# Local attention with a mixture-of-experts step: how many transfers of SyncE's queue are under way at once

## The chip, the cores and the metric

The kernel runs on one core of one Trainium2 chip. A core has TensorE (PE), VectorE (DVE), ScalarE (ACT), GpSimd (POOL) and SyncE (SP), each with its own stream of instructions, and 16 DMA engines that move data between memory (HBM) and the core's SBUF. The metric is device time in microseconds (us) of one execution; less is better.

## The reference

Eight batches of eight heads, 576 positions, head size 64. Attention looks back over 63 positions and the own one. Its output, seen as 576 rows of 512 per batch, is the input of the second part: a gate score per row, the 128 rows of the highest score in each batch go through two dense layers, and the result is added to these rows.

```python
scores = scale * np.matmul(q, k.transpose(0, 1, 3, 2))
mask = (rel >= 0) & (rel < 64)          # rel = query position - key position
attn = softmax(np.where(mask, scores, -1e9))
x = np.matmul(attn, v)                  # then (B, S, H * D): 8, 576, 512
scores = np.einsum('bsd,d->bs', x, w_gate)
for b in range(B):
    top_idx = np.argpartition(-scores[b], 128)[:128]
    xe = x[b, top_idx]
    ye = np.maximum(xe @ w1, 0.0) @ w2  # 512 -> 1024 -> 512
    g = 1.0 / (1.0 + np.exp(-scores[b, top_idx]))
    out[b, top_idx] = x[b, top_idx] + g[:, None] * ye
```

## The kernel before

**Attention.** The 8 x 576 positions are cut into windows of 64, and two windows make one block: 36 blocks of 128 positions with all heads. Block m needs one load of q, one of k and one of v (256 KB each; a k that straddles two batches is two loads of 128 KB). `attend(m)` makes of it: 32 PE instructions of scores (tile s), on DVE the mask and the row maximum (p, nm), on ACT the exponential (p), on PE 8 transposes (t), on ACT the copies to SBUF (pt), on PE the product with v (av, some 60 instructions), on ACT and DVE the division (z, x), on DVE the gate's scalar product, and one store of the 128 rows (x to out_dram, 256 KB; two of 128 KB where a block straddles two batches).

**Mixture of experts.** When the last block of a batch is done, `choose(b)` ranks its 576 scores: PE transposes the scores (r), DVE compares them all with each other, PE sums (lo) and makes the row indices (ix), and POOL gathers the 128 chosen rows from out_dram (xe, an indirect DMA). `moe(gi)` runs the two layers for one or two batches: transposes of the gathered rows (xt), the first layer (hp), transposes of its result (ht), the second layer (yp), the gated sum, and a scatter by POOL. Its weights are split into a high and a low part: `weight(step)` loads one of 16 pieces (st, 256 KB) that POOL splits in two.

**What sets the order.** Nothing in the program is scheduled by the chip's availability at run time: `Order.run` lays all operations out beforehand, engine by engine, by a small model of durations and due times, and emits them in that order; on the chip each engine works its stream off strictly in order, waiting on semaphores. In the model a transfer of SP occupies one common wire (`wire`, `RATE` bytes per us) and lands 1.75 us after its bytes; a transfer isn't issued while the wire is booked more than `BACKLOG` = 3 us ahead:

```python
if op.size and e == "SP":
    t = max(t, wire - BACKLOG)
```

All loads and stores except the first k go through SP's queue, 168 in all. On the chip nothing of this model holds them back: SP issues a transfer as soon as its buffer is free (a q buffer when the scores of an earlier block are done, a store when its x is done) and when its semaphore is free. There are eight semaphores for these transfers, taken in turn (DMAHW0 to DMAHW7; the first k, on ACT's queue, has DMAHW0), so that each transfer waits until the one eight ahead has landed. The loads are written in `load(m)` (`go_q`, `go_k`, `go_k2`, `go_v`), `lwg`, `go_load` and the stores in `go_st`, each as `nc.sync.dma_start`.

Of the kernel before, what the change touches and what calls it, by code (L numbers as in the profile page):

```python
# [12 lines left out]
F32 = _mybir.dt.float32  # L13
# [8 lines left out]
P = 128  # L22
W = 64
# [7 lines left out]
LINK = {"PE": 0.25}  # L31
TURN = 0.15
RATE = 375e3
BACKLOG = 3.0
KEEP = {0: 2, 1: 2, 2: 1}
WARM = 8
DIRECT = (0,)
# [18 lines left out]
class Order:  # L56
# [15 lines left out]
    def add(self, *a, **kw):  # L72
        op = Op(*a, **kw)
        self.ops.append(op)
        return op
# [15 lines left out]
    def run(self, engines, free):  # L91
        for op in self.ops:
            op.left = len(op.after)
            for a, _ in op.after:
                a.then.append(op)
        avail = {e: [] for e in engines}
        for op in self.ops:
            if not op.left:
                avail[op.eng].append(op)
        mode = None  # L100
        wire = 2.0
        done = 0
        self.log = []
        while done < len(self.ops):
            best = None
            for e in engines:
                cand = []
                for op in avail[e]:
                    t, picks = self.ready(op)
                    if t == float("inf"):  # L110
                        continue
                    t = max(t, free[e])
                    if op.size and e == "SP":
                        t = max(t, wire - BACKLOG)
                    cand.append((t, op.due, op, picks))
                if not cand:
                    continue
                t0 = min(c[0] for c in cand)
                same = e == "PE" and mode == 64
                c = min((c for c in cand if c[0] <= t0 + SLACK.get(e, 0.0)  # L120
                         or same and c[2].mode == mode and c[0] <= t0 + STAY),
                        key=lambda c: (same and c[2].mode != mode, c[1]))
                if best is None or c[0] < best[0]:
                    best = c
            assert best is not None, [(e, [o.due for o in avail[e]]) for e in engines]
            t, _, op, picks = best
            if op.mode and mode and op.mode != mode:
                t = max(t, free["PE"] + TURN)
            for (key, kind), n in zip([k for k in op.take if k[0] not in self.where], picks):
                self.where[key] = n  # L130
                self.room[n] = float("inf")
            op.start = t
            if op.mode:
                mode = op.mode
            free[op.eng] = t + op.pitch
            if op.size:
                begin = max(wire, t + op.pitch + 0.25)
                wire = begin + op.size / RATE
                op.end = max(wire, begin + 0.2) + 1.75
            else:  # L140
                op.end = t + op.dur
            for key in op.give:
                self.room[self.where[key]] = op.end + 0.1
            avail[op.eng].remove(op)
            for o in op.then:
                o.left -= 1
                if not o.left:
                    avail[o.eng].append(o)
            self.log.append((t, op))
            op.go()  # L150
            done += 1
# [7 lines left out]
def tile_attention_moe(ctx: ExitStack, tc, q, k, v, wg, w1, w2, outs, B, H, S, D, C):  # L159
    nc = tc.nc  # L160
    E = H * D
    F = w1.shape[1]
    NP = H // 2
# [5 lines left out]
    D1 = D + 1  # L169
    SCALE = 1.0 / np.sqrt(D).item()  # L170
    order = Order()
    add = order.add
# [28 lines left out]
    order.rooms("sel", ["sel0"])  # L201

    serial = [0]

    def make(key, shape, dtype, space="sb", sub=""):
        tag = order.where[key] + sub
        serial[0] += 1
        t = (p_ps if space == "ps" else p_sb).tile(
            shape, dtype, tag=tag, name=f"{key[0]}{sub}{'_'.join(map(str, key[1:]))}")
        order.tiles[key, sub] = t  # L210
        return t

    def get(key, sub=""):
        return order.tiles[key, sub]
# [19 lines left out]
    for opened in (None, 0, 1):  # L234
        m = const.tile([P, 2, W], F32, name=f"mask{len(maskc)}")
        nc.gpsimd.memset(m, 0.0)
        for c in range(2):
            r = slice(c * W, (c + 1) * W)
            nc.gpsimd.affine_select(
                out=m[r, 1, :], in_=m[r, 1, :], pattern=[[-1, W]],  # L240
# [3 lines left out]
            else:  # L244
                nc.gpsimd.affine_select(
                    out=m[r, 0, :], in_=m[r, 0, :], pattern=[[1, W]],
# [57 lines left out]
    wgb = const.tile([P, E], F32, name="wgb")  # L304
# [5 lines left out]
    def at(n, off=0.0):  # L310
        return BEGIN + STEP * n + off
# [9 lines left out]
    def load(m):  # L321
        b, i = divmod(2 * m, NW)
        both = i + 1 == NW
        due = at(m, -9.0)

        def go_q():
            nc.sync.dma_start(make(("q", m), [P, NP, 2, W], F32), q[m])

        def ktile(c):
            if ("k", c) not in order.where or (("k", c), "") not in order.tiles:  # L330
                make(("k", c), [P, NW, NP, W], F32)
            return get(("k", c))

        def go_k():
            eng = nc.scalar if m == 0 else nc.sync
            if not both:
                eng.dma_start(ktile(b)[:, i:i + 2], k[m])
            else:
                eng.dma_start(ktile(b)[:, i], k[m, :, 0])

        def go_k2():
            nc.sync.dma_start(ktile(b + 1)[:, 0], k[m, :, 1])

        def go_v():
            nc.sync.dma_start(make(("v", m), [P, 2, NP, D1], F32), v[m])

        LQ[m] = add("SP", go_q, 0.44, due, take=[(("q", m), "q")], size=P * NP * 2 * W * 4)
        kk = [add("SP", go_k, 0.44, due + 0.01, take=[(("k", b), "k")],
                  size=P * (1 if both else 2) * NP * W * 4)]
        if both:  # L350
            kk.append(add("SP", go_k2, 0.44, due + 0.02, take=[(("k", b + 1), "k")],
                          size=P * NP * W * 4))
        LK[m] = kk
        LV[m] = add("SP", go_v, 0.44, due + (0.03 if m > 1 else 0.6),
                    take=[(("v", m), "vv")], size=P * 2 * NP * D1 * 4)

    for m in range(NM):
        load(m)
    lwg = add("SP", lambda: nc.sync.dma_start(wgb, wg), 0.44, at(1, -7.9), size=P * E * 4)

    w1v = w1.rearrange("(c p) f -> p c f", p=P)
    w2v = w2.rearrange("(c p) e -> p c e", p=P)
    CH = 512
# [3 lines left out]
    def piece(step, t):  # L367
        if step < KC1 * n1:
            j, c = divmod(step, KC1)
            return t[0][:, c, j * CH:(j + 1) * CH]  # L370
        c = (step - KC1 * n1) * n2
        return t[1][:, c:c + n2].rearrange("p a e -> p (a e)")
# [2 lines left out]

    def weight(step):
        def go_load():
            nc.sync.dma_start(make(("st", step), [P, CH], F32), piece(step, (w1v, w2v)))

        def go_hi():  # L380
            nc.gpsimd.tensor_scalar(out=piece(step, (w1h, w2h)), in0=get(("st", step)),
                                    scalar1=1.0, scalar2=1.0, op0=ALU.mult, op1=ALU.mult)

        def go_lo():
            nc.gpsimd.tensor_tensor(
                out=piece(step, (w1l, w2l)), in0=get(("st", step)),
                in1=piece(step, (w1h, w2h)).bitcast(F32), op=ALU.subtract)

        l = add("SP", go_load, 0.44, 12 + 2.2 * step, take=[(("st", step), "h")],
                size=P * CH * 4)  # L390
        WHI[step] = add("POOL", go_hi, 0.62, 16 + 2.2 * step, [l])
        WLO[step] = add("POOL", go_lo, 1.26, 16.1 + 2.2 * step, [WHI[step]],
                        give=[("st", step)])
# [26 lines left out]
    def attend(m):  # L420
# [123 lines left out]
        def xf():  # L544
            return get(("x", m)).rearrange("p j r d -> p (j r d)")
# [10 lines left out]
        b, i = divmod(2 * m, NW)  # L556
# [4 lines left out]

        def go_st(bb, rows, parts):
            def go():
                nc.sync.dma_start(outs[bb][rows, :], xf()[parts])
            return go

        ST[m] = []
# [482 lines left out]
```

## Time and profile before

| | us |
|---|---|
| three runs, median (lowest to highest) | 259.08 (256.22 to 260.87) |
| the profiled execution | 256.81 |
| its span, first to last instruction | 255.1 |
| PE busy in the span | 233.7 |
| DVE busy | 175.4 |
| ACT busy | 157.1 |
| POOL busy | 76.8 |

Busy times are sums over the span; a line number (L512) is that of the kernel before, and a name such as av<-v,pt says what is written from what. The chain that ended last is followed back from the last instruction: at each step to what released it. "issue" in it is time in which an engine waited for nothing that the profile shows. The DMA row has 40 slices of 6.4 us each. A transfer's landing is counted from the start of its issue. A window's row gives, for each engine, busy us and the number of instructions in it.

### The profile page before, as it was taken

Reading aid. Unit: us, or ns where it says so; the run is one execution under the profiler, and the core shown is the slowest. Engines: PE = TensorE matmul, PEld = TensorE weight load, DVE = VectorE, ACT = ScalarE, POOL = GpSimd, SP = SyncE. Lnnn points to the kernel's source line nnn. Section 1 sums busy time; section 2 is a strip of 40 time slices with the busy share of each in tenths; the row PEclk is TensorE's granted clock in tenths of the full one; section 3 lists DMA queues with packets and bytes.
Section 4 is the critical chain, followed back from the end, with each engine's and each line's share of the span. In section 5 each row is a group of like instructions: output and inputs, shape, how many; then the busy total and the mean of one; then the engine's idle time right before and its main releaser. Section 6 shows DMA issues by size and latency. Waiting matters only on the chain.

```text
span 255.1 us, 10922 instructions
## 1 busy us (share of the span) xinstructions
PE 233.7 (92%) x4406; PEld 200.8 (79%) x4406; DVE 175.4 (69%) x911; ACT 157.1 (62%) x451; POOL 76.8 (30%) x117
## 2 busy tenths in 40 slices
PE   8887777987998998999999999999999999999992
PEld 7676756866887887888787878888878899889891
DVE  0588795995797889777997779899765852512210
ACT  2978883974788949777895888799675212101100
POOL 7589967900010025125002500700250030020021
PEclk9999995997999999999999999999999999999998
DMA  7999999984177839943895597363213010011011
GB/s 231 391 387 383 342 319 362 358 309 164 51 237 278 223 117 273 328 127 127 242 344 190 167 326 232 93 183 101 78 66 117 9 58 28 0 44 41 0 44 41
DMA packets 25170, 47.26 MB, mean 185 GB/s; under 512 B 2976, under 2 KB 4000, under 8 KB 25120
## 3 DMA queue, kind: packets, MB, share of 16 engines
q1 hardware_dynamic: 23680, 42.10, 49.4%
q0 software_dynamic: 1296, 4.20, 4.7%
q8 instruction: 35, 0.57, 0.9%
q10 hardware_dynamic: 144, 0.26, 0.3%
q14 instruction: 15, 0.12, 0.1%
HBM read 35.01 MB, written 11.53 MB: 182 GB/s over the span
## 4 chain that ended last, share of the span: by engine, by line
PE 79%; DVE 7%; ACT 5%; issue 4%; DMA 3%; POOLq 0%; ACTq 0%; DVEq 0%
PE yp L965 16%; PE s L430 13%; PE av L512 12%; PE t L468 12%; PE hp L918 9%; PE hp L853 8%; ACT p L460 3%; PE r L615 2%; DMA xe<-out_dram,idx 2%; DVE p L451 2%; PE xt L785 2%; PE wp L221 1%; ACT pt L476 1%; PE ht L882 1%; DMA out_dram<-xe,idxh 1%
## 5 line engine op out<-in xcount | busy, mean ns | idle before, releaser
L460 ACT ACTIVATE p<-p,nm 128x128 f32<-128x128 f32 x288 | 96.3, 398 | 27.1 <-DVE nm L451 27.0
L451 DVE CUSTOM_DVE_ANT_0 p<-s,mask 128x128 f32<-128x128 f32 x288 | 66.1, 282 | 21.4 <-PE s L430 21.1
L512 PE MATMUL av<-v,pt 64*64 64x65 f32 x2176 | 45.0, 225 | 8.8 <-issue 7.1
L512 PEld LDWEIGHTS av<-v,pt 64*64 64x64 f32 x2176 | 41.1, 137 | 12.6 <-issue 9.7
L468 PE MATMUL t<-ident,p 128*128 128x128 f32 x288 | 44.8, 281 | 2.5 <-ACT p L460 1.5
L430 PE MATMUL s<-k,q 64*64 64x128 f32 x1152 | 42.6, 280 | 1.5 <-DVE nm L451 1.1
L430 PEld LDWEIGHTS s<-k,q 64*64 64x64 f32 x1152 | 32.8, 135 | 10.8 <-issue 7.3
L476 ACT COPY pt<-t 128x512 f32<-128x512 f32 x72 | 39.2, 585 | 2.0 <-PE t L468 1.2
L468 PEld LDWEIGHTS t<-ident,p 128*128 128x128 f32 x288 | 32.9, 142 | 7.7 <-ACT p L460 2.5
L997 POOL DMA_INDIRECT out_dram<-xe,idx x7 | 7.9, 1126 | 95.5 <-DVE xe L988 59.5
L414 DVE CUSTOM_DVE_ANT_0 jk<-x,wgb 128x512 bf16<-128x512 f32 x36 | 27.2, 755 | 1.0
L965 PE MATMUL yp<-w2l,hh 128*128 128x512 f32 (+1 forms) x72 | 27.6, 384 | 0.0
L965 PE MATMUL yp<-w2h,hh 128*128 128x512 f32 (+1 forms) x72 | 27.5, 382 | 0.0
L965 PE MATMUL yp<-w2h,hl 128*128 128x512 f32 (+1 forms) x72 | 27.1, 377 | 0.0
L540 DVE TENSOR_TENSOR x<-av,z 128x512 f32<-128x512 f32 x36 | 24.8, 690 | 1.4
L451 DVE DVE_READ_ACCUMULATOR2_ANT nm<- 128x1 f32 x288 | 23.6, 82 | 0.0
L942 ACT ACTIVATE hh<-hp 128x512 fp32r<-128x512 f32 x8 | 4.8, 598 | 28.9 <-PE hp L918 28.9
L760 POOL DMA_INDIRECT xe<-out_dram,idx x8 | 8.8, 1103 | 40.7 <-DVE nm L451 32.3
L532 ACT ACTIVATE z<-av,eps 128x8 f32<-128x8 f32 x36 | 9.4, 260 | 15.0 <-PE av L512 12.3
L918 PE MATMUL hp<-xgh,w1h 128*128 128x256 f32 x64 | 18.2, 284 | 0.0
L918 PE MATMUL hp<-xgh,w1l 128*128 128x256 f32 x64 | 18.2, 284 | 0.0
L918 PE MATMUL hp<-xgl,w1h 128*128 128x256 f32 x64 | 17.9, 280 | 0.0
(97 smaller groups left out, 352.1 us busy)
## 6 DMA issues: line engine op xcount, KB each, us to landing
v<-in_v SPq DMA_DIRECT2D x36, 260.0 KB, 4.0
q<-in_q SPq DMA_DIRECT2D x36, 256.0 KB, 4.3
out_dram<-x SPq DMA_DIRECT2D x32, 256.0 KB, 4.5
k<-in_k SPq DMA_DIRECT2D x31, 256.0 KB, 6.0
st<-in_w SPq DMA_DIRECT2D x16, 256.0 KB, 5.7
k<-in_k SPq DMA_DIRECT2D x8, 128.0 KB, 4.8
out_dram<-x SPq DMA_DIRECT2D x8, 128.0 KB, 4.4
k<-in_k ACTq DMA_DIRECT2D x1, 256.0 KB
```

What stands on the lines that cost most here:

```text
L414: nc.vector.tensor_tensor_reduce(out=junk()[:n, :E], in0=xf[:n], in1=wgb[:n], op0=ALU.mult, op1=ALU.add, scale=1.0, scalar=0.0, accum_out=acc)
L430: nc.tensor.matmul(s[r][c * W:(c + 1) * W, j], get(("q", m))[rs, j, c], keys(m, c, j, rs), start=True, stop=True)
L451: nc.vector.tensor_tensor_reduce(out=get(("p", m))[:, j, :, r], in0=st_s[m][r][:, j], in1=mk, op0=ALU.add, op1=ALU.min, scale=-SCALE, scal ...
L460: nc.scalar.activation(pe[:, j, :, r], pe[:, j, :, r], AF.Exp, bias=st_nm[m][:, r, j:j + 1], scale=-1.0)
L468: nc.tensor.transpose(get(("t", m, a))[:, j, :], get(("p", m))[:, j, a].rearrange("p r w -> p (r w)"), ident)
L476: nc.scalar.copy(pt, get(("t", m, a)))
L512: nc.tensor.matmul(av[cs, r, j * D1:(j + 1) * D1], pt[a][rs, j, cs], get(("v", g // 2))[rs, g % 2, j], start=a == 0 or o == c, stop=a == 1)
L532: nc.scalar.activation(z[:, 0], avv()[:, :, :, D], AF.Identity, bias=eps)
L540: nc.vector.tensor_tensor(out=x.rearrange("p j r d -> p r j d"), in0=avv()[:, :, :, :D], in1=st_z[m][:, 1].unsqueeze(3).to_broadcast([P, 2 ...
L853: nc.tensor.matmul(get(hk)[:C], get(xk, a)[:, c, 0], w[:, c, nb * 512:(nb + 1) * 512], start=(n == 0), stop=(n == 3 * KC1 - 1))
L918: nc.tensor.matmul(get(hk)[:, j], w[:, c, js], get(xk, a)[:, c].rearrange("p u c -> p (u c)"), start=(n == 0), stop=(n == 3 * KC1 - 1))
L965: nc.tensor.matmul(get(yk)[:C, :e1 - e0], get((a, gi, c // per))[:, c % per, u * C:(u + 1) * C], w[:, c, e0:e1], start=(n == 0), stop=(n = ...
```

## The change

From its eleventh transfer on, SP waits before each of its loads and stores until the fourth one ahead on the same queue has landed, so that at most four are under way. The wait is added by hand (`move`), and the planner's model gets the same rule in place of `BACKLOG`. All transfers of SP's queue now go through `move`.

```diff
-BACKLOG = 3.0
+FLIGHT = 4
+FIRST = 10
...
         wire = 2.0
+        flight = []
...
-                    if op.size and e == "SP":
-                        t = max(t, wire - BACKLOG)
+                    if op.size and e == "SP" and len(flight) >= FIRST:
+                        t = max(t, flight[-FLIGHT] + 0.1)
...
                 op.end = max(wire, begin + 0.2) + 1.75
+                if op.eng == "SP":
+                    flight.append(op.end)
...
+    flight = []
+
+    def move(out, in_, eng=None):
+        i = (eng or nc.sync).dma_start(out, in_)
+        if eng is None:
+            if len(flight) >= FIRST:
+                tc.add_manual_dep(
+                    i.ins, flight[-FLIGHT].name,
+                    _mybir.DependencyInfo(_mybir.DependencyClass.Sync,
+                                          _mybir.DependencyReason.DATA),
+                    reason="transfers under way")
+            flight.append(i.ins)
...
-            nc.sync.dma_start(make(("q", m), [P, NP, 2, W], F32), q[m])
+            move(make(("q", m), [P, NP, 2, W], F32), q[m])
```

The other loads and the store are changed like the last two lines.

SP's queue, its tenth to twentieth transfer before the change (q, k, v of a block, st a piece of weights; a number behind a name tells buffers apart), with what each waits for:

```order
L327 DMA q_198<-in_q 128x512 [waits DMAHW2_49]
L337 DMA k_160<-in_k 128x512 [waits DMAHW3_49]
L345 DMA v_215<-in_v 128x520 [waits DMAHW4_49]
L378 DMA st_240<-in_w 128x512 [waits DMAHW5_49]
L378 DMA st_264<-in_w 128x512 [waits DMAHW6_49]
L327 DMA q_278<-in_q 128x512 [waits DMAHW7_49]
L339 DMA k_160<-in_k 128x256 [waits DMAHW0_49]
L342 DMA k_316<-in_k 128x256 [waits DMAHW1_49]
L345 DMA v_323<-in_v 128x520 [waits DMAHW2_49]
L378 DMA st_354<-in_w 128x512 [waits DMAHW3_49]
L378 DMA st_363<-in_w 128x512 [waits DMAHW4_49]
```

The same place of SP's queue after it:

```order
L213 DMA q_254<-in_q 128x512 [waits DMAHW2_49]
L213 DMA k_160<-in_k 128x512 [waits DMAHW7_49,DMAHW3_49]
L213 DMA v_285<-in_v 128x520 [waits DMAHW4_49,DMAHW0_49]
L213 DMA st_312<-in_w 128x512 [waits DMAHW5_49,DMAHW1_49]
L213 DMA st_348<-in_w 128x512 [waits DMAHW6_49,DMAHW2_49]
L213 DMA q_360<-in_q 128x512 [waits DMAHW3_49]
L213 DMA k_160<-in_k 128x256 [waits DMAHW4_49]
L213 DMA k_398<-in_k 128x256 [waits DMAHW5_49]
L213 DMA v_442<-in_v 128x520 [waits DMAHW6_49]
L213 DMA out_dram<-x_369 128x512 [waits DMAHW7_49,DVE_49]
L213 DMA st_462<-in_w 128x512 [waits DMAHW0_49]
```

The tenth transfer waits as before. The eleventh to fourteenth wait for two semaphores, their own (eight ahead) and that of the fourth ahead; from the fifteenth on the fourth ahead is left, since the one eight ahead has been waited for by then. The first store has moved from the 24th to the 19th place. The load of the eighth q (block 7, counted from 0) goes from the 33rd place to the 34th, the last piece of weights from the 59th to the 61st.

PE's stream between the index matmuls (ix) of the second batch and the transposes (xt) of the rows gathered by these indices, its first rows before the change:

```order
L736 MATMUL ix_1609<-posb_137,sel_4_1600 128x2
L468 MATMUL t_0_1619<-ident,p_1488 128x128 [waits PE_49,Activation_49]
L468 MATMUL t_0_1619<-ident,p_1488 128x128 [waits Activation_49] x3
L853 MATMUL hp_1_1399<-w1l,xgh_1114 128x512 [waits Pool_49]
L853 MATMUL hp_1_1399<-w1h,xgl_1115 128x512
L468 MATMUL t_1_1643<-ident,p_1488 128x128 [waits DVE_49]
L468 MATMUL t_1_1643<-ident,p_1488 128x128 x3
L965 MATMUL yp_0_1653<-w2h,hh_0_1432 128x512 [waits Pool_49]
```

and after it:

```order
L754 MATMUL ix_1434<-posb_137,sel_4_1425 128x2
L871 MATMUL hp_1_1376<-w1h,xgh_1088 128x512
L871 MATMUL hp_1_1376<-w1l,xgh_1088 128x512 [waits Pool_49]
L871 MATMUL hp_1_1376<-w1h,xgl_1089 128x512
L983 MATMUL yp_0_1450<-w2h,hh_0_1419 128x512 [waits Activation_49,Pool_49]
L983 MATMUL yp_0_1450<-w2l,hh_0_1419 128x512 [waits Pool_49]
L983 MATMUL yp_0_1450<-w2h,hl_0_1432 128x512 [waits DVE_49]
L983 MATMUL yp_0_1450<-w2h,hh_0_1419 128x512
```

Up to xt there follow, before the change, eight more rows of yp, four transposes ht, the scores of one block and the V product of another. After it, one more of yp, the four of ht, two transposes t, the scores of one block, the V product of another and one transpose t. The rows behind the scores of the last block are the same in both.

## Rows read from the trace of the kernel before

**Rows 1.** The page, busy us of each engine, share of the span, instructions.
```profile
PE 233.7 (92%) x4406; PEld 200.8 (79%) x4406; DVE 175.4 (69%) x911; ACT 157.1 (62%) x451; POOL 76.8 (30%) x117
```

**Rows 2.** The page, GB/s of the DMA engines in 40 slices of 6.4 us.
```profile
GB/s 231 391 387 383 342 319 362 358 309 164 51 237 278 223 117 273 328 127 127 242 344 190 167 326 232 93 183 101 78 66 117 9 58 28 0 44 41 0 44 41
```

**Rows 3.** Chain of work that ended last: start us, us, what.
```profile
15.69 0.99 issue
...
20.38 1.46 issue
...
25.53 1.42 issue
...
56.70 2.38 issue
```

**Rows 4.** Waits of PE, who for whom: us in total, times, longest us.
```profile
PE av L512 <- issue: 7.1, 7, 2.4
...
PE av L512 <- ACT p L460: 1.3, 1, 1.3
...
PE xt L785 <- DMA xe<-out_dram,idx: 1.0, 1, 1.0
```

**Rows 5.** The page, DMA queue 8: packets, MB, share of 16 engines.
```profile
q8 instruction: 35, 0.57, 0.9%
```

**Rows 6.** DMA queue 8 in the windows 24.6 to 24.7, 56.6 to 56.8, 109.8 to 110.0.
```profile
q8 instruction: 1, 0.02, 54.9%
...
q8 instruction: 1, 0.02, 30.1%
...
q8 instruction: 1, 0.02, 31.6%
```

**Rows 7.** Windows: stretch, us, busy us (instructions) per engine, PEclk, DMA share, GB/s.
```profile
20.38:25.53 5.15, 3.69 (x125) 3.28 (x126) 4.42 (x29) 4.01 (x14) 5.15 (x5) 1.00 1.04 381
...
21.84:24.65 2.81, 2.81 (x88) 2.58 (x88) 2.08 (x9) 1.89 (x6) 2.81 (x5) 1.00 1.04 375
59.09:109.90 50.81, 48.55 (x1031) 41.63 (x1031) 41.93 (x221) 39.01 (x113) 7.27 (x8) 0.97 0.63 201
```

**Rows 8.** One q load and one v load on SP: ns of issue, start, landing.
```profile
L327 SPq DMA_DIRECT2D q<-in_q x1: 431/431/431, 21.8 to 21.8; - x1
...
DMA to landing us min/median/max: 5.5/5.5/5.5
...
L345 SPq DMA_DIRECT2D v<-in_v x1: 328/328/328, 170.6 to 170.6; - x1
...
DMA to landing us min/median/max: 2.6/2.6/2.6
```

**Rows 9.** Waits of SP between 5 and 23 us.
```profile
SPq L378 <- DMA v<-in_v: 1.6, 3, 0.7
SPq L345 <- DMA q<-in_q: 0.9, 3, 0.4
```

**Rows 10.** Windows of three attention blocks, and of the stage around 56.7 us.
```profile
14.49:18.79 4.30, 3.31 (x105) 2.93 (x104) 3.75 (x21) 3.52 (x12) 3.80 (x4) 1.00 1.03 389
18.79:23.61 4.82, 3.36 (x106) 2.94 (x105) 4.09 (x21) 3.68 (x12) 4.82 (x6) 1.00 1.06 393
23.61:28.47 4.86, 3.44 (x106) 3.03 (x105) 3.41 (x21) 3.67 (x12) 4.86 (x6) 1.00 1.01 357
55.02:66.58 11.56, 9.18 (x117) 7.90 (x116) 7.08 (x33) 6.93 (x21) 0.00 (x0) 0.85 0.41 140
```

**Rows 11.** Timeline of PE: scores of block 7, start us, us.
```profile
32.04 0.44 PE L430 MATMUL s<-k,q 64*64 64x128 f32 x4
```

**Rows 12.** Chain of work that ended last: a gather, transposes, second-layer matmuls.
```profile
73.27 6.02 DMA xe<-out_dram,idx
...
80.00 0.87 PE t L468 x8
...
88.63 2.09 PE yp L965 x9
```

## What the change does to the time: the prediction

> **What bounds the kernel now.** I read the page first. TensorE (PE) is busy for 92% of the span, VectorE (DVE) 69%, ScalarE (ACT) 62% [rows 1]; matmuls are pipelined, so this alone proves little. The DMA row says that the first 45 us are another stage than the rest: 320 to 390 GB/s once it has begun, later mostly under 300 [rows 2]. Then the chain that ended last. Nearly all of it is PE work, and the few holes in it are the question. The largest are called "issue", time in which PE waited for nothing that the profile shows: 0.99, 1.46 and 1.42 us in the first 27 us and 2.38 us at 56.70, 6.25 us together [rows 3]. In the list of PE's waits they are the first row, 7.1 us before the probability-times-V matmuls; behind it come one wait of 1.3 us put down to ACT and one of 1.0 us for a gather [rows 4]. All other holes have an engine or a gather to name.
>
> What ends the "issue" holes? The loads and stores show a queue of the kind "instruction": 35 packets, 0.57 MB, so 16 KB each [rows 5]. In narrow windows one packet can be placed in time: its share times window times 16 engines is its length. The packet that starts between 24.6 and 24.7 takes 54.9% x 0.1 x 16 = 0.88 us and ends near 25.53, where a hole begins; the one that starts between 56.6 and 56.8 takes 0.96 us and ends near 57.7, inside the hole from 56.70 to 59.09 [rows 3, 6]. In both, PE goes on about 1.4 us after the packet has ended. From the start of one hole to the start of the next, PE did 125 matmuls and 126 weight loads [rows 7], 251 instructions; 16 KB of 64 bytes is 256, and a few semaphore instructions make up the rest. So I read it thus: PE's program arrives in 16 KB blocks, and in the holes PE has run out of instructions.
>
> The Trainium skill (Runtime: NRT & Kernel Launch, section Instruction fetch mechanics) has the same 16 KiB blocks of 256 instructions, and says that crossing to the next one is mostly hidden. The trace agrees on the size, by its 251 instructions, and not on the hiding, by its 6.25 us.
>
> Why are some blocks late? With little else under way the packet came early: one starts between 109.8 and 110.0 us, and by 109.90 PE had done 2062 instructions since the hole that ended at 59.09, which is 8.2 blocks; so the packet started when a fifth of the block in hand was used, and no hole followed. In the crowded stretch, from 21.84 to the packet at 24.65, PE had used 176 of 251, seven tenths [rows 6, 7]. The same request thus waits some microseconds longer when SyncE's (SP's) queue is full. A q load issued at 21.8 took 5.5 us to land; a v load with the queue nearly empty, at 170.6, took 2.6 us [rows 8]. At 391 GB/s one 256 KB transfer takes 0.67 us of the wire [rows 2], and eight of them 5.4 us: the 5.5 us is the queue of eight that the kernel allows itself, since each transfer reuses the semaphore of the one eight ahead (the order's rows on SP). SP waited for such landings all through this stretch [rows 9]. A block that is fetched through an engine with this backlog waits behind it.
>
> **The change, part by part.** (1) *The waits.* From SP's row 11 on, each transfer waits for the one four ahead; most of the old waits, eight ahead, fall away as implied. No instruction is added that computes. Queued behind a waiting transfer are the next loads and stores of SP, nothing else. With four under way the backlog is 4 x 0.67 = 2.7 us, about the lone landing of 2.6 us, so landing falls from 5.5 to between 2.7 and 3.0 us (an estimate: 2.6 us and one issue of SP, 431 ns [rows 8], in front). A block then starts some 2.5 us earlier. The holes of 0.99, 1.46 and 1.42 us need less than that, the 2.38 us just that.
>
> What this is worth is read stage by stage. Three blocks of attention, 14.49 to 28.47, take 13.98 us; PE is busy for only 3.31 to 3.44 us of each, but DVE for 3.75, 4.09 and 3.41 and ACT for 3.52 to 3.68 [rows 10]. Without holes the pace is set by these two, whose work of a block depends on each other; I take 4.0 us a block, 12.0 in all. So 3.87 us of holes give 2.0 us (between 0, if DVE and ACT take it all back, and 2.7, at DVE's mean of 3.75 us a block). In the stage around 56.70 PE has work of its own, 9.18 us in 11.56 us, against 7.08 for DVE [rows 10]: that hole counts nearly whole, 2.2 us (0 to 2.4). The 1.3 us put down to ACT has the same line and comes in the middle of the same matmuls; it could be such a hole or not, so half, 0.6 us (0 to 1.3). The smaller "issue" holes in the row of 7.1 us, 0.9 us beyond the four: 0.2 us (0 to 0.9). Sum 5.0 us (0 to 7.3).
>
> (2) *Does the window starve the transfers?* Four landings in 2.7 to 3.0 us are 0.68 to 0.75 us a transfer instead of 0.67. The tightest use I found is the eighth q load: issued at 21.8, landed 5.5 us later at 27.3, used at 32.04 [rows 8, 11], 4.8 us to spare. It is SP's 34th row after the change, so 23 waits lie before it: 23 x 0.08 = 1.8 us late at the most, inside the 4.8. Cost 0; without that cover, 1.8 us.
>
> (3) *The planner's order.* The planner now believes in later landings, so it moves rows on every engine. The PE work is the same and the rows behind the last attention blocks are the same, so only covers change. The one I can price: between the index matmuls of the second sequence and the transposes of the rows gathered by them, PE had two first-layer and nine second-layer matmuls and eight transposes of probabilities beside one block's scores and one V product; now it has three, five and three (the order's rows on PE show the first of them). A matmul of these is 2.09 / 9 = 0.23 us, a transpose 0.87 / 8 = 0.11 us [rows 12], so 3 x 0.23 + 5 x 0.11 = 1.2 us of cover is gone, in a place where PE waited 1.0 us for a gather of 6.02 us [rows 4, 12]. A shorter backlog should shorten that gather by about as much. I take a loss of 0.4 us (0 to 1.2). Stores move ahead of weight loads on SP, which costs nothing: they go out once their block is done, and weight pieces are first used long after.
>
> Sum: 5.0 - 0.4 = 4.6 us. The profiled execution took 256.81 us (span 255.1), so 252.2 for one like it; the median of the three is 259.08, 2.3 us above, and one like it would come to 254.5. Holes that depend on the phase of a queue may well differ between executions, so I lean to the lower one: **253.0 us**.
>
> **The rivals.** *The holes close but the time is taken back* by DVE and ACT, by new, shorter holes (a block that meets four transfers still waits 2.7 us, and its last 0.9 + 1.4 us come on top), or by the new order: gain 0 to 3 us, 256 to 259 us. For it: DVE and ACT at 3.5 to 4.1 us of each early block. Against it: the stage at 56.70, where PE alone is short.
>
> *The blocks do not wait behind the transfers.* Then nothing changes but the order: 257 to 260 us. For it, the trace has no row that shows when a block is asked for. Against it, a fifth against seven tenths of a block used. The Trainium skill (DMA: Bandwidth & Descriptors, section Queues, rings and completion order) says that an engine goes round its queue rows packet by packet; by that a block would wait for one packet and not for a queue, and the change would give nothing. The late packets in the crowded stretch speak against it here.
>
> *Slower: the window starves the loads.* If landing does not shorten with the depth, four in 4.4 us (towards the middle between 3.0 and 5.5) are 1.1 us a transfer: 23 x (1.1 - 0.67) = 9.9 us late at the eighth block, 4.8 us of it to spare, 5.1 us of waits: 262 us. It decides from 0.67 + 4.8 / 23 = 0.88 us a transfer, 3.5 us for four. Against it: 2.6 us for a lone one.
>
> **How the numbers follow.** The forecast, holes mostly gone and the sum about right: 0.57. Time taken back: 0.25. Blocks not behind the transfers: 0.08. Starved loads: 0.10. A measurement of this kernel can tell about 2% from no change, 5.2 us, so faster means under 253.9. The forecast's own range is 249.5 to 255.5, of which I put 0.9 under 253.9, and a sliver of the second case: faster 0.54. Slower, over 264.3, needs most of the starving or a bad order: 0.07. Same 0.39. The range for 8 in 10 goes from 248.8 (all 7.3 us from the profiled execution, and 0.7) to 259.0.
>
> **What would show it.** Right: no "issue" hole over 0.5 us on PE in the first 60 us; landing of a q load near 22 us about 3 us; a block's packet that starts when less than half of the block in hand is used; the DMA row still near 350 GB/s in the first 40 us; attention blocks of about 4.0 us there. Wrong: holes of the same size with the shorter queue (blocks do not wait behind it); score matmuls that wait for loads, and DMA under 280 GB/s (starved); a gather wait of over 2 us (the order).

## The result: 1.0% slower, with the holes nearly gone

Median 258.75 us over 20 runs (256.49 to 262.70), against 257.62 us over 20 runs of the kernel before (254.06 to 262.86): ratio 1.0104, 95% interval 1.0069 to 1.0139. Executions more than 1.5% above the fastest of the same kernel are left out of the ratios, so a ratio in this text is not the quotient of the medians beside it. The profiled execution has a span of 257.6 us, against 255.1 before.

The page of the kernel after: PE's busy time, the granted clock in 40 slices of 6.4 us in tenths, and the GB/s of the DMA engines (the rows that answer [rows 1, 2]).

```profile
PE 235.6 (91%) x4406; PEld 201.6 (78%) x4406; DVE 175.5 (68%) x911; ACT 157.4 (61%) x451; POOL 76.6 (30%) x117
...
PEclk9999599599999999999999999999999999999999
...
GB/s 237 320 219 253 276 285 245 275 250 281 238 296 270 266 218 189 283 275 198 247 273 224 267 277 285 123 135 121 51 81 84 41 45 41 0 43 41 0 43 41
```

Waits of PE after, who for whom: us in total, times, longest us (these answer [rows 4]).

```profile
PE s L448 <- DMA k<-in_k: 5.5, 3, 3.4
PE t L486 <- ACT p L478: 2.2, 3, 1.0
PE xt L803 <- DMA xe<-out_dram,idx: 1.7, 2, 1.5
...
PE s L448 <- issue: 0.9, 1, 0.9
PE av L530 <- issue: 0.8, 3, 0.3
```

Two things happened at once. The wait for "issue" before the V products fell from 7.1 us [rows 4] to 0.8, none longer than 0.3 us: the holes of [rows 3] are gone. One "issue" wait of 0.9 us is left ahead of score matmuls, at 98.4 us; all rows of "issue" together fell from 7.8 to 1.9 us. And a wait that was not there before stands on top of the list: the score matmuls wait 5.5 us for k loads. The DMA row of the page tells where it comes from: 219 to 285 GB/s from the third to the ninth slice, where it was 309 to 387 [rows 2].

PE's timeline after, between 14 and 27 us: start us, us, what, and in brackets the idle time ahead of it and what ended it.

```profile
14.29 1.10 PE L448 MATMUL s<-k,q 64*64 64x128 f32 x32
...
19.33 0.99 PE L448 MATMUL s<-k,q 64*64 64x128 f32 x27 [1.41 <-DMA k<-in_k]
...
25.75 2.10 PE L448 MATMUL s<-k,q 64*64 64x128 f32 x32 [3.37 <-DMA k<-in_k]
```

Blocks 4 and 5 wait for their k. During the second wait the granted clock falls from 1.00 to a half (1.2 instead of 2.4 GHz), and the same 32 score matmuls take 2.10 us instead of 1.10. (Before, the clock falls once between 10 and 58 us, near 38.6; after, twice, near 24.5 and 45.0.) How the first stage pays for this is one row of each kernel, the window from 10 to 60 us (stretch, us, busy us and instructions of each engine, PEclk, DMA share, GB/s); the kernel before first:

```profile
10.00:60.00 50.00, 40.06 (x1027) 33.75 (x1026) 39.50 (x222) 36.38 (x110) 32.97 (x35) 0.92 0.99 349
```

The same window after:

```profile
10.00:60.00 50.00, 40.17 (x946) 33.92 (x945) 35.47 (x207) 34.63 (x104) 29.60 (x32) 0.86 0.84 259
```

As much busy time, but 946 matmuls instead of 1027, at a clock of 0.86 instead of 0.92, with 259 GB/s instead of 349. Over the whole profiled execution PE's busy time grew by 1.9 us for the same 4406 matmuls, and the sum of the listed waits from 15.8 to 16.3 us; together 2.4 of the 2.5 us by which the spans differ.

By the records of SP's instructions, transfers 11 to 61 are issued between 8.93 and 59.41 us, 50 steps of 1.01 us (before: 11 to 59 between 5.82 and 41.08 us, 48 steps of 0.73 us). How long they took to land stands in the DMA issues of a window (what, count, KB each, median us from issue to landing). The trace has the landing of one transfer in eight only, so each of these medians rests on one or two transfers (from 3.5 to 4.7 us after, from 5.0 to 5.7 before). After, from 10 to 60 us:

```profile
st<-in_w SPq DMA_DIRECT2D x16, 256.0 KB, 4.0
...
k<-in_k SPq DMA_DIRECT2D x7, 256.0 KB, 4.1
out_dram<-x SPq DMA_DIRECT2D x6, 256.0 KB, 3.5
```

and before, from 6 to 41 us:

```profile
st<-in_w SPq DMA_DIRECT2D x15, 256.0 KB, 5.7
...
q<-in_q SPq DMA_DIRECT2D x8, 256.0 KB, 5.2
```

Half as many under way landed in about 0.7 of the time, not in half of it.

### The profile page after: what moved, and what is told of

The parts are those of the page before. It is cut to its first block, busy times and chain, and to the rows that moved or that the text cites. A ratio compares the mean times of both kernels' runs of the same rounds, so it can differ in the third digit from the quotient of the medians.

```text
span 257.6 us, 10912 instructions
## 1 busy us (share of the span) xinstructions
PE 235.6 (91%) x4406; PEld 201.6 (78%) x4406; DVE 175.5 (68%) x911; ACT 157.4 (61%) x451; POOL 76.6 (30%) x117
## 4 chain that ended last, share of the span: by engine, by line
PE 65%; DMA 3%; DVE 2%; issue 2%; ACT 1%; POOLq 0%; ACTq 0%
PE yp L983 16%; PE s L448 10%; PE t L486 9%; PE av L530 9%; PE hp L936 9%; PE hp L871 6%; DMA xe<-out_dram,idx 2%; PE r L633 2%; PE xt L803 1%; DVE p L469 1%; DMA out_dram<-xe,idxh 1%; PE ht L900 1%; PE lo L713 1%; ACT p L478 1%; POOLq L1064 0%
## 5 line engine op out<-in xcount | busy, mean ns | idle before, releaser
L469 DVE CUSTOM_DVE_ANT_0 p<-s,mask 128x128 f32<-128x128 f32 x288 | 66.5, 282 | 31.4 <-PE s L448 31.1
L448 PE MATMUL s<-k,q 64*64 64x128 f32 x1152 | 45.1, 286 | 8.0 <-DMA k<-in_k 5.5
L486 PE MATMUL t<-ident,p 128*128 128x128 f32 x288 | 46.5, 286 | 3.5 <-ACT p L478 2.2
L448 PEld LDWEIGHTS s<-k,q 64*64 64x64 f32 x1152 | 34.6, 139 | 18.3 <-issue 11.1
L530 PE MATMUL av<-v,pt 64*64 64x65 f32 x2176 | 44.4, 226 | 0.9 <-issue 0.8
L530 PEld LDWEIGHTS av<-v,pt 64*64 64x64 f32 x2176 | 41.7, 139 | 3.7 <-issue 2.4
L1015 POOL DMA_INDIRECT out_dram<-xe,idx x7 | 7.3, 1047 | 81.6 <-DVE xe L1006 59.3
L432 DVE CUSTOM_DVE_ANT_0 jk<-x,wgb 128x512 bf16<-128x512 f32 x36 | 26.2, 728 | 1.0
L739 POOL TENSOR_SCALAR sel<-slots,diff 128x128 bf16<-128x128 f32 x20 | 14.6, 735 | 27.6 <-DVE diff L723 26.8
L1006 DVE SCALAR_TENSOR_TENSOR xe<-yp,gs,xe 128x512 f32<-128x512 f32 (+1 forms) x9 | 6.2, 692 | 16.5 <-PE yp L983 16.5
```

Source lines behind the costliest of these rows:

```text
L432: nc.vector.tensor_tensor_reduce(out=junk()[:n, :E], in0=xf[:n], in1=wgb[:n], op0=ALU.mult, op1=ALU.add, scale=1.0, scalar=0.0, accum_out=acc)
L448: nc.tensor.matmul(s[r][c * W:(c + 1) * W, j], get(("q", m))[rs, j, c], keys(m, c, j, rs), start=True, stop=True)
L469: nc.vector.tensor_tensor_reduce(out=get(("p", m))[:, j, :, r], in0=st_s[m][r][:, j], in1=mk, op0=ALU.add, op1=ALU.min, scale=-SCALE, scal ...
L486: nc.tensor.transpose(get(("t", m, a))[:, j, :], get(("p", m))[:, j, a].rearrange("p r w -> p (r w)"), ident)
L530: nc.tensor.matmul(av[cs, r, j * D1:(j + 1) * D1], pt[a][rs, j, cs], get(("v", g // 2))[rs, g % 2, j], start=a == 0 or o == c, stop=a == 1)
L739: (nc.vector if soon else nc.gpsimd).tensor_scalar(out=sel[r], in0=(slots if t < NT - 1 else slots2)[r], scalar1=st["diff"][r, t:t + 1], s ...
```

## The experiments

The theories after this result: (A) with four under way the transfers are starved in the first stage, and this takes back what the closed holes give. Rivals: (B) the planner's new order is to blame and the waits are not; (C) the loads are slow because PE or the order is in their way, not because there are only four.

**The two halves of the change apart.** The waits on the order of before, that is the planner's old rule put back into the kernel after:

```diff
+BACKLOG = 3.0
...
-                    if op.size and e == "SP" and len(flight) >= FIRST:
-                        t = max(t, flight[-FLIGHT] + 0.1)
+                    if op.size and e == "SP":
+                        t = max(t, wire - BACKLOG)
```

> The waits of the change (fourth one ahead, from the eleventh transfer on) with the order of the kernel before: the planner keeps its old rule. Theory A (the waits starve the early loads: the four under way land only when the slowest of the 16 DMA engines has caught up, so a transfer takes 1.0 us instead of 0.73): PE waits for q and k loads at blocks 4 to 8 as in the changed kernel, DMA 250 to 290 GB/s in the first 45 us, time like the changed kernel or worse, 258 to 262 us. Theory B (the new order of the rows loses the time): no worse than before, 252 to 257 us, since the instruction holes close.

Measured: 264.76 us, ratio 1.0336 (1.0253 to 1.0419). Its largest waits of PE, and the row of the timeline with the longest:

```profile
PE xt L804 <- DMA xe<-out_dram,idx: 6.5, 2, 5.9
PE s L449 <- DMA k<-in_k: 5.9, 3, 2.6
PE av L531 <- issue: 3.2, 6, 1.1
```

```profile
57.81 0.47 PE L804 MATMUL xt<-ident,xe 128*128 128x128 f32 x1 [5.88 <-DMA xe<-out_dram,idx]
```

Against before, k waits of 5.9 us are new, the gather costs 5.5 us more and "issue" 3.9 us less: 7.5 of the 8.8 us between the two spans (PE's busy time, 235.0 us, holds another 1.3). The gather is late because the stores that it reads from stand in the same line: in the order of before, the last two stores ahead of it are the 48th and 49th transfers on SP; at 1 us apiece they go out from 49.31 us on, and the gather is issued at 52.6 us, 10 us after its index matmuls. Before, it is issued at 40.0 us, and in the kernel after, whose order has these stores at places 43 and 44, at 46.1; in both that is 0.9 us after the index matmuls.

The new order without the waits, which is one line of the kernel after:

```diff
-            if len(flight) >= FIRST:
+            if False:
```

> The order of the changed kernel without its added waits: SP waits again only for the transfer eight ahead. Theory A: transfers of 0.73 us, no wait of PE for a load of blocks 4 to 8, the issue holes of 1 to 2.4 us back, 255 to 259 us, about like before. Theory B: 258 to 262 us, like the changed kernel or worse, as the holes are back and the order is the new one.

Measured: 259.24 us, ratio 1.012 (1.0048 to 1.0192). No score waits for a load, and the "issue" waits are back. Its waits of PE, and the window from 10 to 60 us:

```profile
PE av L530 <- issue: 5.5, 6, 1.9
PE xt L803 <- DMA xe<-out_dram,idx: 2.3, 2, 1.3
PE t L486 <- ACT p L478: 1.6, 2, 1.0
```

```profile
10.00:60.00 50.00, 41.06 (x953) 34.63 (x951) 36.99 (x216) 35.20 (x105) 32.78 (x35) 0.86 0.86 284
```

So the order alone costs 3.1 us (1.2 to 4.9), and it is not seen where I had looked for it: the sum of the listed waits is 15.7 us, as before (15.8). In the profiled execution the loss is in PE's busy time, 236.5 us against 233.7, for the same matmuls, at a mean granted clock of 0.968 against 0.977; the difference lies in this window (0.86 against 0.92). Over the executions that the ratio compares, the mean clock is 0.976 here and 0.984 before, for which the difference would come to (0.9836 - 0.9756) x 258 = 2.1 us, an estimate.

One place where the clock falls, in PE's timeline of this kernel:

```profile
28.19 0.56 PE L530 MATMUL av<-v,pt 64*64 64x65 f32 x19 [1.93 <-issue]
28.68 1.09 PE L486 MATMUL t<-ident,p 128*128 128x128 f32 x8
30.81 0.69 PE L486 MATMUL t<-ident,p 128*128 128x128 f32 x2 [1.03 <-ACT p L478]
31.43 1.99 PE L448 MATMUL s<-k,q 64*64 64x128 f32 x32
```

The same place before:

```profile
26.95 0.56 PE L512 MATMUL av<-v,pt 64*64 64x65 f32 x19 [1.42 <-issue]
27.45 1.09 PE L468 MATMUL t<-ident,p 128*128 128x128 f32 x8
28.47 1.10 PE L430 MATMUL s<-k,q 64*64 64x128 f32 x32
```

The planner, which believes that block 6's loads come late, has put two transposes of block 5 ahead of block 6's scores. Those wait for ACT, and the scores behind them start at 31.4 us, at half the clock; the order of before starts them at 28.5. Of these 3.0 us, 1.2 were there ahead of the two transposes (28.68 against 27.45), from longer "issue" holes. Nor does the clock fall here under the new order alone. The kernel with waits from the 62nd transfer only (below) has the order of before and no added wait in this stage; in its profiled execution, with "issue" holes of 1.8, 1.5 and 2.0 us, the same scores come late and slow too:

```profile
30.85 1.99 PE L449 MATMUL s<-k,q 64*64 64x128 f32 x32
```

That the order costs 3.1 us is measured; what in it does so is not shown.

The start of each block's first score matmul (us, from the four traces) sets the halves side by side:

| block | before | after | waits alone | order alone |
|---|---|---|---|---|
| 4 | 18.8 | 17.5 | 19.0 | 19.3 |
| 5 | 23.6 | 25.8 | 23.2 | 24.3 |
| 6 | 28.5 | 32.9 | 30.4 | 31.4 |
| 9 | 45.9 | 50.9 | 50.7 | 50.2 |
| 12 | 66.6 | 71.9 | 75.0 | 70.6 |
| 35 | 184.7 | 187.6 | 193.5 | 187.9 |

On the old order the waits cost 3.4%. On the new one they change little, 1.0104 with them and 1.012 without: there the k waits (5.5 us) and the "issue" waits that go (from 8.2 to 1.9 us in all rows) about cancel. So A and B both hold, each for a part.

**How many under way.** In both the waits and the planner, FLIGHT of six, then of three:

```diff
-FLIGHT = 4
+FLIGHT = 6
```

> Six instead of four, in the waits and in the planner. Theory A: six under way cover a landing of about 4 us, so a transfer takes at most 0.75 us, PE waits for no load, DMA is over 340 GB/s in the first 40 us; the issue holes shrink by half, 254 to 257 us. Theory B: a third order, so anything between 254 and 260 us, with no loads late either way.

Measured: 256.21 us, ratio 0.9992 (0.9948 to 1.0037). The profiled execution took 257.62 us.

```profile
PE av L530 <- issue: 5.3, 7, 1.5
PE xt L803 <- DMA xe<-out_dram,idx: 3.8, 2, 2.1
```

No score waits for a load. "Issue" before the V products is hardly less than without a window; in all rows it is 5.8 us against 8.2.

> Three instead of four, in the waits and in the planner. Theory A: a transfer takes 1.1 to 1.3 us (a landing of 3.3 to 3.9 us over three), PE waits for loads up to block 12 and later, 262 to 275 us. Theory B: 256 to 261 us, as the loads are late by little.

Measured once: 263.18 us, span 261.5. Transfers 11 to 61 go out 1.16 us apart.

```profile
PE t L486 <- ACT p L478: 6.1, 6, 2.1
PE s L448 <- DMA k<-in_k: 2.7, 2, 1.4
```

The k wait in the rows is smaller than with four, probably because this planner has moved still more PE work ahead of the loads; the transposes wait 6.1 us for ACT instead, and PE is busy for 237.5 us. "Issue" before the V products is 2.3 us here, more than with four; but most of it is not at the end of a block of PE's program (the table in the next section).

**Where the waits hurt.** The order of before with waits of four from the 62nd transfer only, then the opposite, from the 11th to the 61st only (here and below the planner has its old rule back, as above; those lines are not shown again):

```diff
 FLIGHT = 4
-FIRST = 10
+FIRST = 61
```

> The order of the kernel before, and the waits for the fourth one ahead only from the 62nd transfer of SP on, when all weights have been asked for. Theory A (four under way starve only the stage that is bound by transfers): the early holes stay, no load is late, since block 12 and later had their q 18 us and more ahead; the hole of 2.4 us near 57 and the one of 1.3 us near 101 shrink, 253 to 256.5 us. Rival (the window costs wherever it is, because loads then wait behind stores): 258 to 262 us.

Measured: 253.68 us, ratio 0.9892 (0.9835 to 0.9949).

```diff
-            if len(flight) >= FIRST:
+            if FIRST <= len(flight) < 61:
```

> Order of the kernel before; a transfer waits for the fourth ahead from the eleventh to the sixty-first only, the later ones wait for nothing. If the loss of the waits on this order (8.6 us) is all from the starved first part, and the later waits gain some 2 to 3 us: 266 to 268 us, with xt waiting for its gather 5 us or more and the scores for k 4 us or more. If the window costs by being there throughout (the later loads as well): clearly under 264.8, about 261.

Measured: 265.55 us, ratio 1.0337 (1.0269 to 1.0405), the same as with the waits to the end (1.0336).

```profile
PE xt L804 <- DMA xe<-out_dram,idx: 5.8, 2, 5.2
PE av L531 <- issue: 3.0, 5, 1.7
PE s L449 <- DMA k<-in_k: 3.0, 2, 2.4
```

All of the loss is made by the waits on the first 61 transfers. What the later waits give was less clear, so three more kernels. The order of before with six under way from the 11th on:

> The order of the kernel before, and waits for the sixth one ahead from the eleventh transfer on. Theory A: a transfer takes at most 0.75 us, no load is late, the issue holes are about half of what they were and the gather waits stay near 1 us, 254 to 256.5 us. Rival (any window makes loads late in the old order): 258 to 262 us.

Measured: 255.54 us, ratio 0.9973 (0.9933 to 1.0013). The same with four from the 62nd on:

```diff
-                    i.ins, flight[-FLIGHT].name,
+                    i.ins, flight[-FLIGHT if len(flight) < 61 else -4].name,
```

> Order of the kernel before; a transfer waits for the sixth ahead from the eleventh to the sixty-first, and for the fourth ahead from the sixty-second on. If the loss of four under way sits in the first 61 transfers alone, where loads are used soon after they land, and the later ones lose nothing: the two gains add (six from the eleventh was 0.997 of before, four from the sixty-second 0.989), 253 us, between 251 and 255, no wait of the scores for a load, gather wait of xt under 1 us. If the 0.989 was mostly a matter of when the blocks of the first part came by chance (the trace shows the same holes before av as before, 7.1 us): 255 to 257, no different from six alone.

Measured: 256.17 us, ratio 0.9981 (0.9936 to 1.0025); the two gains did not add. And the kernel with four from the 62nd once more:

> The kernel of e5_old_order_four_from_62 once more, unchanged. e5 alone was 0.989 of before, but with six under way ahead of it (e8) the same late waits gave nothing (0.998), and on this order four from the eleventh with and without the late waits are equal (264.8 and 265.6). If four under way from the sixty-second on is a gain of its own: 0.985 to 0.993 again, 253 to 254.5 us. If e5 was the favourable end of a scatter that this kernel has from run to run: 0.995 to 1.002, 255.5 to 257.5 us, and the later waits count as worth nothing that these runs can tell.

Measured: 255.09 us, ratio 0.9945 (0.9895 to 0.9994). It is faster than the kernel before in each of its two measurements, by 1.1 and 0.5%, the second between the two ranges that I had set apart; the traces don't settle why. The holes of the first stage are all there (5.4 us of "issue" before the V products in the last one), as nothing was changed there. Between 60 and 120 us it gains: 1292 matmuls are done there in the last one's profiled execution, 1197 before; but the kernel with six and then four does 1288 there, and it is no faster than before over its runs. That four from the 62nd on are harmless is shown; that they are a gain of their own is likely, not more.

**The transfers by themselves.** A kernel with nothing but loads of 256 KB, 32 of them to a stretch, with eight, six, five, four, three and two under way, PE idle, and then some stretches beside a stream of matmuls (nothing of the reference is computed):

```diff
+    for window in (8, 6, 5, 4, 3, 2):
+        g = stretch(window, 32)
```

> Nothing of the reference is computed, the outputs are zeros. 32 loads of 256 KB on SP's queue with 8, 6, 5, 4, 3 and 2 under way in turn, while PE is idle; then 32 each with 8, 6 and 4 beside a PE that runs a stream of matmuls as dense as the attention's. Theory A1 (a landing of four is long because one DMA engine falls behind whenever it brings PE's next instructions): four under way take 0.67 to 0.72 us a transfer with PE idle, 0.9 to 1.0 us beside the stream; eight take 0.65 to 0.75 in both. Theory A2 (the landing is simply longer than I read from one load, whatever PE does): four take 0.85 to 1.0 us in both, three 1.1 to 1.3, two 1.5 to 1.8. Rival (it is the waits and stores of the kernel): four take 0.67 to 0.72 us in both.

Measured: windows of it, for eight, six, five, four, three, two under way with PE idle, then for eight and four beside matmuls (stretch, us, busy us and instructions of PE, PEld, DVE and POOL, PEclk, DMA share, GB/s):

```profile
8.00:20.00 12.00, 0.00 (x0) 0.00 (x0) 0.00 (x0) 0.00 (x0) 1.00 1.05 393
32.00:46.00 14.00, 0.00 (x0) 0.00 (x0) 0.00 (x0) 0.00 (x0) 1.00 1.00 361
57.00:75.00 18.00, 0.00 (x0) 0.00 (x0) 0.00 (x0) 0.00 (x0) 1.00 0.94 307
86.00:106.00 20.00, 0.00 (x0) 0.00 (x0) 0.00 (x0) 0.00 (x0) 1.00 0.90 290
118.00:141.00 23.00, 0.00 (x0) 0.00 (x0) 0.00 (x0) 0.00 (x0) 1.00 0.83 262
150.00:185.00 35.00, 0.00 (x0) 0.00 (x0) 0.00 (x0) 0.00 (x0) 1.00 0.65 195
197.00:213.00 16.00, 16.00 (x299) 13.83 (x301) 0.00 (x0) 0.00 (x0) 1.00 1.03 382
...
284.00:300.00 16.00, 16.00 (x300) 13.78 (x289) 0.00 (x0) 0.00 (x0) 1.00 0.85 262
```

and the landing with eight and with four under way, PE idle:

```profile
b<-in_q SPq DMA_DIRECT2D x18, 256.0 KB, 5.4
```

```profile
b<-in_k SPq DMA_DIRECT2D x18, 256.0 KB, 3.6
b<-in_q SPq DMA_DIRECT2D x4, 256.0 KB, 3.9
```

Four under way carry 290 GB/s, 0.90 us a transfer, with PE idle, and 262, 1.0 us, beside matmuls; eight lose almost nothing beside matmuls (393 and 382). So A holds against C for the larger part: alone, a transfer goes from 0.68 to 0.90 us, 0.22 more, and in the kernel it went from 0.73 to 1.01, 0.28 more. A lone load lands in 2.5 us here, four under way in 3.6 to 3.9. The landings, engine by engine, show where the rest is. A transfer is spread over 16 DMA engines and has landed when the last of them is done. For the last two loads, each alone, the median engine is done after 2.4 us and the last 0.1 us later; with four under way it is 2.8 us and 3.8. Every new wait hangs on that last one, while the others run dry: the DMA share is 0.90 and not 1.05. The kernel after shows it at the k of block 5, for which PE waits longest: by the updates of its semaphore 15 of its engines are done by 24.19 us, the last at 25.62.

## Why the prediction was wrong

**The mechanism: right.** The holes of [rows 3] were blocks of PE's program that came late behind SP's loads and stores; before the V products they went from 7.1 to 0.8 us with the shorter queue. Without the waits, on the very same order, they are 5.5 us. The instruction records, which I had not counted through, make the reading firmer. PE's program counted from its start, weight loads and semaphore instructions included, each of the 31 "issue" holes over 0.7 us in the eleven traces (all but the kernel of loads) ends with 193 or 194 instructions beyond a multiple of 256 ahead of it, that is at the same place in a block of 16 KB. The 1.3 us put down to ACT [rows 4], of which the sum took half, end there too. The packet with the next block started, on the mean of the first 60 us, 3.3 us after PE had begun the block in hand before the change, 1.4 us after the change, and 2.5 with the order alone.

The holes put down to "issue" at these places alone, us in all:

| transfers under way | eight (no wait) | six | four | three |
|---|---|---|---|---|
| order of before | 6.8 | 6.7 | 3.0 | |
| new order, planned for this depth (under eight: for four) | 7.2 | 5.0 | 1.2 | 0.6 |

The shorter the queue, the less is left. It is not the queue alone: where PE waits for loads, a block gains time as well. For the early holes this was little. Of the second block after the change, the packet ended at 17.92 us; with the 1.4 us that passed from packet to PE in the holes before, it would have been some 0.2 us late without PE's k wait of 1.41 us (20.50 - 1.41 = 19.09; an estimate).

So the rival that blocks do not wait behind the transfers is not borne out: waits taken away and put back moved the holes with them. That rival could lean on the Trainium skill (DMA: Bandwidth & Descriptors, section Queues, rings and completion order), by which an engine goes round its queues packet by packet; these runs do not agree with a block's waiting for one packet only.

**Step 2, "does the window starve the transfers?", failed**, and with it the sign. I put landing with four under way at 2.7 to 3.0 us, from a lone load's 2.6 us, as if a transfer's 16 engines stayed in step; a lone load could not show that they don't. A wait ends with the slowest of them. Landing took 3.5 to 4.7 us in the kernel where the trace has it, and SP's transfers were 1.0 us apart, past the 0.88 us that the prediction itself named as the point from which the slower rival decides. The use that I called tightest, the eighth q load with 4.8 us to spare, was not the tightest either: block 5's k is SP's 23rd row, issued at 20.50 us, 11.6 us after the eleventh at 8.93 instead of 12 x 0.67 = 8.0, landed at 25.62, and the scores took it at 25.75. The rival's price, 5.1 us of waits, was close to the 5.5 us that came, by luck: it was worked out for the eighth q, and the waits came at the k of blocks 4 and 5 (4.8 us) and once at 61 us (0.7).

**Forecast and rivals came true together.** I had made them alternatives. The rival's sum went without the gain of the holes (262 us), the forecast's without the loss of the loads (253), and the kernel got both: 258.75. A shorter queue that lets the blocks through sooner is the same shorter queue that carries less, and the sum needed both terms at once. "Time taken back" had named the new order too, without a price for it. That 258.75 us lies inside the range up to 259.0 is luck: its upper end stood for holes that close and for DVE and ACT taking the time back, not for late loads.

**Step 3, the planner's order, was mis-sized:** 0.4 us (0 to 1.2) was put down, for the cover of one gather; 3.1 us were measured (1.2 to 4.9), by the order alone. The gather did wait somewhat longer (2.3 us instead of 1.0), but the sum of all waits did not grow. In the profiled execution the loss came as PE work at the lower clock, 2.8 us, and a sum of waits has no term for that; over all the executions compared the clock accounts for some 2.1 us. Why this order brings more time at the lower clock stays open.

**The gain of the closed holes** was put at 5.0 us. It can't be read on its own, since no kernel closed the holes without starving the loads. On the new order the waits take away 6.3 us of "issue" (8.2 to 1.9) and bring 5.5 us of k waits, and the time differs by (1.012 - 1.0104) x 257.62 = 0.4 us in their favour, less than the intervals tell apart; so the holes were worth about as much as the loads cost.

**What I had said would show it.** "No issue hole over 0.5 us" in the first 60 us held: there is none at all. A block's packet that starts before half of the block in hand is used came from the second block on (0.48, 0.38, 0.17; before 0.73, 0.71, 0.83), the last of these at half the clock. (The "fifth" that the prediction read off at 109.8 us is 36 of 256, a seventh; nothing hangs on it.) Landing of about 3 us, a DMA row near 350 GB/s and attention blocks of about 4.0 us did not (blocks 4 and 5 took 8.3 and 7.1 us from scores to scores). Score matmuls that wait for loads and DMA under 280 GB/s, named as the sign of starved loads, came both. The gather wait stayed under 2 us in one piece (1.5), as hoped, and the order cost time anyway.

## To carry to other kernels

A window on transfers under way has a price that a lone transfer's landing doesn't tell: time a stretch of the real transfers at that depth first, with nothing beside it, and compare us a transfer with the spare time of each early load, the first tight one above all. When one cause (here the depth of the queue) sets both the gain and the loss, put both in the sum and don't keep them as separate cases. Where a planner re-orders the work, its cost may lie in the granted clock and not in the waits: compare busy time and matmuls done in a fixed window, and the clock over several executions.

## What the runs showed of the hardware that I had not expected

- Rate by the number of 256 KB loads under way on SP's queue, PE idle: 393, 361, 307, 290, 262 and 195 GB/s for eight, six, five, four, three and two.
- PE's program arrives in blocks of 256 instructions, and a block came later with eight transfers under way on SP's queue than with four: its packet started 3.3 us after the block in hand was begun in the kernel before and 2.5 with the order alone, eight under way in both, and 1.4 with four.
- The spread over the 16 DMA engines: in the kernel after, the last engine of a transfer is done 0.5 us after the median one where no block of PE's program is fetched meanwhile (47 transfers), 1.1 us where one is (110 transfers), medians by the semaphores' updates. A block is a single packet of 16 KB, 0.9 to 1.7 us long, and it would hold up one engine of the sixteen. It fits the drop from 290 to 262 GB/s beside matmuls. That it is the cause was not tried.
- The two stretches with six and four under way beside matmuls in the kernel of loads had a stall ahead of them, loads that waited for a buffer; it lies outside the windows shown.
